# The first loads of a fused retention and SwiGLU kernel: constants moved to ScalarE's queue, their product moved behind the first scores, fewer unread products

## The chip, the cores and the metric

The kernel runs on one core of one Trainium2 chip. The core has TensorE (PE: products, PEld: its weight loads), VectorE (DVE), ScalarE (ACT), GpSimd (POOL) and SyncE (SP), which here only issues transfers; ScalarE can issue transfers too. The metric is the time of one execution on the device in microseconds (us), median of three runs.

## What is computed

Block-wise retention over 4 sequences of 768 rows with 8 heads of width 64, and then a gated feed-forward block (3072 rows, width 512, inner width 1536) over its output:

```python
for b in range(nb):                       # blocks of 64 rows
    qb, kb, vb = q[:, :, sl], k[:, :, sl], v[:, :, sl]
    intra = einsum('bhic,bhjc->bhij', qb, kb) * Dmask
    intra = einsum('bhij,bhjd->bhid', intra, vb)
    inter = einsum('bhid,bhde->bhie', qb * lam_pow, kv_state)
    out[:, :, sl] = intra + inter
    kv_state = lam_block * kv_state + einsum('bhsd,bhse->bhde', kb * rev_pow, vb)
...
rms = sqrt(mean(x * x, axis=-1) + 1e-6)
xn = x / rms * rms_g
g = xn @ w_gate
silu = g * (1.0 / (1.0 + exp(-g)))
return (silu * (xn @ w_val)) @ w_out
```

Here `lam` has one decay per head; `Dmask`, `lam_pow` and `rev_pow` are powers of it.

## The kernel before

**Tiling.** The 3072 rows are cut into 6 groups of 512. The heads are taken in 4 pairs, so a pair of heads fills 128 partitions. For each group and pair one tile `qkv` holds q and k across (half of the tile, called qK here) and k and v along (the other half, kv), each half 512 KB. The kernel uses chunks of 128 rows, four to a group.

**A pair's steps** (class `Pair`, lines 457 to 578). TensorE computes the scores `pa` from qK (line 477). VectorE multiplies them by the decay `mask` of each of the two heads into `a` (L497). ScalarE multiplies k by the last column of the masks (`decay_k`, L487). TensorE then makes the state sums `pst` from the decayed k and v (L510) and VectorE chains them into `state` (L523, L525). GpSimd multiplies q by `pw` (`decay_q`, L501). TensorE adds `a` times v and then the old state times the decayed q into `po` (`mix_chunks` L538, `mix_states` L549). ScalarE copies `po` away (`keep_output`, L561) and squares it (`keep_squares`, L572); GpSimd adds the squares of the first three pairs (L578), and TensorE sums them over the partitions into `pss` (L589) for the row norm.

**Constants.** A small tile `cs` (128 partitions of 64 bytes, 8 KB) holds the heads' decays and the norm's gain. VectorE makes from it eight masks (L153) and four `pw` (L158), each by a scan over 128 columns, and the largest gain `gmax` (L173), which TensorE spreads over the partitions by one product, `pmax` (L179); from that VectorE makes the scales `gs` (L183 to L189).

**Loads.** Before anything else the program issues `cs` (L67), the four pairs of group 0 (L96) and the first weights (L108). All go out from SyncE but one: the first pair's qK goes out from ScalarE (line 95). Both queues end in the same DMA engines. The pairs of the next group are issued from SyncE as soon as tiles come free.

**The order of the work** is written out by a planner (class `Plan`, lines 1089 to 1254). Each step has an engine, a cost, a due time, what it reads and writes. `arrive_steps` (line 1499) enters the landing of the first loads as steps with costs, `ramp_steps` (line 1510) the work on the first two groups. The table `SHIFTS` (line 1760) moves the due times of some 850 of 2730 steps. `Plan.run` goes through the steps and writes down, engine by engine, the order in which they are issued; on the chip each engine works through its instructions in that order and waits on semaphores.

**Unread products.** Where the planner sees TensorE idle for more than 0.8 us before the first Strassen unit, the loop at the end puts in products of the identity with itself, whose result nobody reads (`busy`, line 140; line 1969 sets how many). A product of float32 operands shows in the trace as two MATMUL records.

Of the kernel before, what the change touches and what calls it, by code (L numbers as in the profile page):

```python
# [22 lines left out]
def retention_swiglu_kernel(  # L23
# [11 lines left out]
    nc = tc.nc  # L35

    NG, NP = qkv.shape[:2]
# [28 lines left out]
    cs = const.tile([P, NC], F32, name="cs")  # L66
    nc.sync.dma_start(cs, consts)  # L67
# [55 lines left out]
    for p in range(NP):  # L123
        load_qkv(0, p)
# [1139 lines left out]
    step = plan.add  # L1264
# [234 lines left out]
    def arrive_steps():  # L1499
        def arrive():  # L1500
            pass

        step("LD", 4.3, -9, arrive, w=["cs", "come"])
        times = [0.75, 1.3, 1.55, 1.35, 1.85, 1.3, 1.3, 1.3]
        for p in range(NP):
            for i, c in enumerate(("qK", "kv")):
                step("LD", times[2 * p + i], -9, arrive, w=["come", *[f"q0_{p}:{x}" for x in c]])
        step("LD", 3.05, -9, arrive, w=["come", "gv0"])
# [234 lines left out]
    def load_steps():  # L1743
# [138 lines left out]
    with tc.manual_schedule(  # L1882
# [78 lines left out]
        for t, i in order:  # L1961
            eng, cost, _, fn, args, _, _, new, _ = plan.steps[i]
            begun = len(traced)
            if eng == "PE":
# [3 lines left out]
                if gaps and idle > 0.8:  # L1968
                    busy(int((idle - 0.5) / 0.24))
# [81 lines left out]
```

## Time and profile before

| | us |
|---|---|
| median of three runs | 631.17 (630.66 to 631.37) |
| profiled execution | 629.99 |
| its span, first to last instruction | 628.2 |
| TensorE busy in the span | 622.2 |

The profile is of one execution; its times start at the span's start. Busy time of TensorE is from modelled ends of its products, so a stretch in which it is busy throughout may still hold short waits. The rows that matter are in the section before the prediction.

### The profile page before, as it was taken

What the parts mean: (1) busy time and instruction counts of PE and PEld (TensorE: products, weight loads), DVE (VectorE), ACT (ScalarE), POOL (GpSimd) and SP (SyncE); (2) the same over time, 40 slices, a digit from 0 to 9 for tenths busy, and PEclk for the clock granted to TensorE, in tenths of its full rate; (3) what the DMA queues carried; (4) which work ended last, traced back from release to release, by engine and by line L of the source; (5) the groups of instructions that cost most, each with busy time, mean ns of one, the idle gap of its engine ahead of it and who ended that gap; (6) DMA issues with size and microseconds to landing.
All of it is one profiled execution on the core that took longest, in us unless ns stands there. A gap on an engine that the chain in (4) does not pass through costs nothing.

```text
span 628.2 us, 14174 instructions
## 1 busy us (share of the span) xinstructions
PE 622.2 (99%) x5665; PEld 479.3 (76%) x5665; DVE 452.8 (72%) x886; ACT 383.9 (61%) x724; POOL 127.6 (20%) x113
## 2 busy tenths in 40 slices
PE   9999999999999999999999999999999999999997
PEld 8864444455657777668888888888889888888886
DVE  6889888777787778788875789634874778546641
ACT  3779799986546764568764685534853564445531
POOL 3531201142825665410020110011000110000000
DMA  8899898888646788878878667744675667343401
GB/s 320 305 318 299 313 313 290 288 279 290 231 148 226 258 284 273 275 265 284 269 268 297 216 212 225 244 179 152 226 224 179 202 207 248 109 135 105 148 18 51
DMA packets 56033, 144.05 MB, mean 229 GB/s; under 512 B 5920, under 2 KB 18208, under 8 KB 54560
## 3 DMA queue, kind: packets, MB, share of 16 engines
q1 hardware_dynamic: 55824, 142.64, 67.3%
q8 instruction: 44, 0.72, 0.5%
q10 hardware_dynamic: 144, 0.52, 0.3%
q14 instruction: 21, 0.17, 0.1%
HBM read 106.96 MB, written 36.18 MB: 228 GB/s over the span
## 4 chain that ended last, share of the span: by engine, by line
PE 94%; DMA 2%; DVE 1%; ACT 1%; SPq 0%; issue 0%; POOL 0%; ACTq 0%; POOLq 0%
PE o L1050 20%; PE pa L779 20%; PE pb L779 15%; PE pv L668 9%; PE pg L668 9%; PE o L938 5%; PE pa L477 4%; PE po L538 3%; PE po L549 3%; DMA qkv<-in_qkv_dram 2%; PE o_own L1050 2%; PE pst L510 2%; PE pss L589 1%; PE unread L144 1%; PE pr L630 0%
## 5 line engine op out<-in xcount | busy, mean ns | idle before, releaser
L779 PEld LDWEIGHTS <-gw 128*128 128x128 f16 x1440 | 139.5, 98 | 21.9 <-issue 0.8
L1050 PE MATMUL o<-wo,late 128*128 128x256 f16 x1152 | 143.9, 273 | 0.5 <-ACT late L1061 0.5
L1050 PEld LDWEIGHTS <-late 128*128 128x128 f16 x1260 | 123.0, 98 | 15.1 <-issue 0.8
L668 PEld LDWEIGHTS <-w_half 128*128 128x128 f16 x576 | 53.9, 98 | 60.5 <-issue 1.5
L833 ACT COPY tx<-pa 128x256 f32<-128x256 f32 x96 | 35.3, 371 | 72.9 <-PE pa L779 55.5
L779 PE MATMUL pa<-tx,gw 128*128 128x256 f16 x576 | 77.4, 273 | 0.0
L668 PE MATMUL pv<-x,w_half 128*128 128x512 f16 x288 | 69.2, 379 | 0.2
L668 PE MATMUL pg<-x,w_half 128*128 128x512 f16 x288 | 66.8, 379 | 0.0
L837 DVE TENSOR_TENSOR tx<-pb,tx 128x256 f32<-128x256 f32 x96 | 40.0, 420 | 31.4 <-PE pb L779 29.1
L779 PEld LDWEIGHTS <-gv 128*128 128x128 f16 x576 | 56.0, 98 | 7.4 <-issue 0.2
L501 POOL TENSOR_TENSOR qkv<-qkv,pw 128x512 f32<-128x512 f32 x24 | 30.6, 1275 | 74.8 <-PE pa L477 66.5
L845 DVE TENSOR_TENSOR sg<-pb,sg 128x256 f32<-128x256 f32 x48 | 20.1, 422 | 35.4 <-ACT sg L841 30.7
L1013 DVE TENSOR_TENSOR late<-s,late 128x1024 f16<-128x1024 f32 x30 | 37.3, 1253 | 5.2 <-ACT late L1009 5.1
L708 POOL TENSOR_TENSOR r<-w_half 128x512 f32<-128x512 f16 x24 | 27.7, 1163 | 63.3 <-DVE w_half L440 25.5
L497 DVE TENSOR_TENSOR a<-pa,mask 128x512 f32<-128x512 f32 x48 | 31.4, 683 | 12.0 <-PE pa L477 8.5
L779 PE MATMUL pa<-x,gv 128*128 128x256 f16 x288 | 39.3, 273 | 0.0
L779 PE MATMUL pb<-x,gv 128*128 128x256 f16 x288 | 39.3, 273 | 0.0
L779 PE MATMUL pa<-x,gw 128*128 128x256 f16 x288 | 39.0, 273 | 0.0
L779 PE MATMUL pb<-tx,gw 128*128 128x256 f16 x288 | 39.0, 273 | 0.0
L779 PE MATMUL pb<-x,gw 128*128 128x256 f16 x288 | 38.7, 273 | 0.0
L938 PE MATMUL o<-wo,early 128*128 128x512 f16 x144 | 34.9, 379 | 0.0
L729 POOL TENSOR_TENSOR ws<-ws,ws 128x512 f16<-128x512 f32 x24 | 28.8, 1210 | 29.3 <-DVE en L325 15.3
(152 smaller groups left out, 1031.0 us busy)
## 6 DMA issues: line engine op xcount, KB each, us to landing
gw<-gw_kept SPq DMA_DIRECT2D x48, 640.0 KB, 4.8
qkv<-in_qkv_dram SPq DMA_DIRECT2D x47, 512.0 KB, 6.0
h<-h_kept SPq DMA_DIRECT2D x30, 512.0 KB, 4.1
h_kept<-sg SPq DMA_DIRECT2D x48, 256.0 KB, 3.4
gv<-gw_kept SPq DMA_DIRECT2D x48, 256.0 KB, 4.4
raw_gv<-in_weights_dram SPq DMA_DIRECT2D x11, 1024.0 KB, 7.2
raw_o<-in_weights_dram SPq DMA_DIRECT2D x24, 256.0 KB, 4.4
gw_kept<-ws SPq DMA_DIRECT2D x12, 512.0 KB, 4.2
```

The source lines that it names most:

```text
L477: nc.tensor.matmul(self.pa[j][:, c, :], self.kT[r, c, :], self.qT[r, c, :], start=True, stop=True,)
L497: nc.vector.tensor_mul(self.a[:, j], self.pa[j], decay)
L501: eng.tensor_mul(self.qT, self.qT, pw[:, p : p + 1, :].broadcast_to([P, GC, P]))
L668: nc.tensor.matmul(ps, w[:, kk, :], x[:, kk, :], start=i == kk == 0, stop=i == 2 and kk == NK - 1,)
L708: nc.gpsimd.tensor_add(self.r[:, i], w[:, 0], w[:, 1])
L729: eng.tensor_sub(self.to[:, c, 1], self.t[:, c], self.to[:, c, 0])
L779: nc.tensor.matmul(ps, w(ow, k), x(ox, k), start=first and i == k == 0, stop=i == 2 and k == 1, skip_group_check=True,)
L833: nc.scalar.copy(self.val_sums[:, self.half(t)], self.pa)
L837: nc.vector.tensor_add(v, self.pb, v)
L938: nc.tensor.matmul(self.banks[t], h[:, oh, t * P : (t + 1) * P], wo[:, j, 3 + 2 * k : 5 + 2 * k, ow], start=j == k == i == 0, stop=j == HA ...
L1013: eng.tensor_sub(lo, of, hi)
L1050: nc.tensor.matmul(bank[:, t], ops[:, oh, t * P : (t + 1) * P], w[:, ow], start=n in (1, 2, 5) and q == i == 0 and (t == 0 or bank is own) ...
```

## The change

The constants' transfer leaves the head of SyncE's queue, and is issued by ScalarE behind the first pair's qK. The planner's table of landings is replaced, with the landing of `cs` behind that of the first qK. The divisor that sets the number of unread products goes from 0.24 to 0.4. `SHIFTS` is replaced as a whole, which moves steps throughout the program.

```diff
     cs = const.tile([P, NC], F32, name="cs")
-    nc.sync.dma_start(cs, consts)
     lam_b, lam_p, gcol = cs[:, :H], cs[:, H : H + NP], cs[:, H + NP :]
...
-    for p in range(NP):
+    load_qkv(0, 0)
+    nc.scalar.dma_start(cs, consts)
+    for p in range(1, NP):
         load_qkv(0, p)
     load_gv(0)
...
-        step("LD", 4.3, -9, arrive, w=["cs", "come"])
-        times = [0.75, 1.3, 1.55, 1.35, 1.85, 1.3, 1.3, 1.3]
+        times = [5.0, 1.0, 1.6, 1.4, 1.6, 1.3, 1.3, 1.6]
         for p in range(NP):
             for i, c in enumerate(("qK", "kv")):
                 step("LD", times[2 * p + i], -9, arrive, w=["come", *[f"q0_{p}:{x}" for x in c]])
+                if p == i == 0:
+                    step("LD", 0.1, -9, arrive, w=["come", "cs"])
...
     SHIFTS = {
-        14: 13.03, 16: 14.75, 17: 15.55, 18: 16.43, 19: 19.96, 20: 21.25, 21: 18.22, 22: 18.97,
+        14: 13.01, 16: 14.72, 17: 15.58, 18: 16.46, 19: 20.01, 20: 21.3, 21: 18.25, 22: 19.03,
...
                 if gaps and idle > 0.8:
-                    busy(int((idle - 0.5) / 0.24))
+                    busy(int((idle - 0.5) / 0.4))
```

On TensorE, at the start of the program, the order before is this (`pa_0` are the scores of the first pair of heads, `pst_0` its state sums, `po_0` its output; `pa_1` and so on are the second pair's):

```order
L144 MATMUL unread<-ident 128x128 x10
L179 MATMUL pmax<-ident,gmax 128x128
L477 MATMUL pa_0_0_214<-qkv_0_145 128x128
...
L477 MATMUL pa_0_1_215<-qkv_0_145 128x128
L144 MATMUL unread<-ident 128x128 x3
L510 MATMUL pst_0_238<-qkv_0_145 64x64 x8
L538 MATMUL po_0_249<-a_0_228,qkv_0_145 64x128 x8
L477 MATMUL pa_1_0_262<-qkv_1_148 128x128
```

and of the changed kernel, at the same place, this:

```order
L145 MATMUL unread<-ident 128x128 x7
L478 MATMUL pa_0_0_205<-qkv_0_144 128x128
L478 MATMUL pa_0_1_206<-qkv_0_144 128x128
L478 MATMUL pa_0_0_205<-qkv_0_144 128x128
L478 MATMUL pa_0_1_206<-qkv_0_144 128x128
L180 MATMUL pmax<-ident,gmax 128x128
...
L511 MATMUL pst_0_227<-qkv_0_144 64x64 x8
L478 MATMUL pa_1_0_237<-qkv_1_148 128x128
...
L539 MATMUL po_0_245<-a_0_224,qkv_0_144 64x128 x4
```

The constants' product has moved from ahead of the first pair's scores into their middle, three unread products are gone ahead of them and three behind them, and the first half of the second pair's scores has moved ahead of the first pair's output. One more unread product, ahead of `pss`, is gone too: 14 before, 7 now.

On VectorE, at its first instructions, the order before is this (`mask` and `pw` are the scans over the constants, `a_0` the first pair's masked scores, the last row the second pair's):

```order
L173 TENSOR_REDUCE gmax<-cs 128x1
L153 SCALAR_TENSOR_TENSOR mask<-cs,ident 128x128 x2
L158 SCALAR_TENSOR_TENSOR pw<-cs,w_half_96 128x128
L153 SCALAR_TENSOR_TENSOR mask<-cs,ident 128x128 x2
L158 SCALAR_TENSOR_TENSOR pw<-cs,w_half_96 128x128
L153 SCALAR_TENSOR_TENSOR mask<-cs,ident 128x128
L497 TENSOR_TENSOR a_0_228<-pa_0_0_214,mask 128x512
L497 TENSOR_TENSOR a_0_228<-pa_0_1_215,mask 128x512
...
L153 SCALAR_TENSOR_TENSOR mask<-cs,ident 128x128 x2
L158 SCALAR_TENSOR_TENSOR pw<-cs,w_half_96 128x128
L497 TENSOR_TENSOR a_1_283<-pa_1_0_262,mask 128x512
```

and of the changed kernel this:

```order
L174 TENSOR_REDUCE gmax<-cs 128x1
L154 SCALAR_TENSOR_TENSOR mask<-cs,ident 128x128 x4
L159 SCALAR_TENSOR_TENSOR pw<-cs,w_half_95 128x128
L498 TENSOR_TENSOR a_0_224<-pa_0_0_205,mask 128x512
L498 TENSOR_TENSOR a_0_224<-pa_0_1_206,mask 128x512
L159 SCALAR_TENSOR_TENSOR pw<-cs,w_half_95 128x128
...
L498 TENSOR_TENSOR a_1_264<-pa_1_0_237,mask 128x512
L154 SCALAR_TENSOR_TENSOR mask<-cs,ident 128x128 x2
L159 SCALAR_TENSOR_TENSOR pw<-cs,w_half_95 128x128
L154 SCALAR_TENSOR_TENSOR mask<-cs,ident 128x128
L498 TENSOR_TENSOR a_1_264<-pa_1_1_238,mask 128x512
```

Five scans instead of seven stand ahead of the first pair's masked scores, and three masks and a `pw`, among them the mask that the second pair's second head waits for, have moved between the two halves of the second pair's masked scores.

On TensorE again, at the end of the four pairs of group 0 (`po_1` to `po_3` are their outputs, `pst` the state sums, `pss` the sums of squares for the norm), the order before is this:

```order
L538 MATMUL po_1_314<-a_1_283,qkv_1_148 64x128 x8
L549 MATMUL po_1_314<-qkv_1_148,state 64x128 x6
L477 MATMUL pa_3_0_335<-qkv_3_154 128x128
...
L510 MATMUL pst_2_342<-qkv_2_151 64x64 x8
L538 MATMUL po_2_353<-a_2_319,qkv_2_151 64x128 x8
...
L549 MATMUL po_2_353<-qkv_2_151,state 64x128 x6
L510 MATMUL pst_3_382<-qkv_3_154 64x64 x8
L538 MATMUL po_3_397<-a_3_379,qkv_3_154 64x128 x8
L144 MATMUL unread<-ident 128x128
L589 MATMUL pss_421<-ones,sq_304 128x1 x4
```

and of the changed kernel this:

```order
L539 MATMUL po_1_298<-a_1_264,qkv_1_148 64x128 x8
L478 MATMUL pa_2_0_276<-qkv_2_151 128x128
...
L550 MATMUL po_1_298<-qkv_1_148,state 64x128 x6
L511 MATMUL pst_2_327<-qkv_2_151 64x64 x8
L478 MATMUL pa_3_0_338<-qkv_3_154 128x128
...
L539 MATMUL po_2_356<-a_2_324,qkv_2_151 64x128 x8
L550 MATMUL po_2_356<-qkv_2_151,state 64x128 x6
L539 MATMUL po_3_382<-a_3_362,qkv_3_154 64x128 x8
L511 MATMUL pst_3_398<-qkv_3_154 64x64 x8
L590 MATMUL pss_411<-ones,sq_284 128x1 x4
```

The second half of the third pair's scores (`pa_2`) now stands behind the second pair's output, and the unread product ahead of `pss` is gone. On ScalarE, the constants' transfer has come in ahead of the table load, and the squares of the first and the third pair now stand ahead of the copies of their outputs.

## Rows read from the trace of the kernel before

**Rows 1.** The page's first part: busy time, share of the span and instructions of each engine.

```profile
PE 622.2 (99%) x5665; PEld 479.3 (76%) x5665; DVE 452.8 (72%) x886; ACT 383.9 (61%) x724; POOL 127.6 (20%) x113
```

**Rows 2.** Busy time by stretch: the stretch, its length, then busy time and instructions of PE, PEld, DVE, ACT and POOL, the granted TensorE clock, the share of the DMA engines and GB/s.

```profile
0.00:6.00 6.00, 4.54 (x22) 4.51 (x22) 1.20 (x5) 1.69 (x3) 1.41 (x11) 1.00 0.65 202
...
60.00:620.00 560.00, 559.53 (x4992) 432.97 (x4991) 402.97 (x771) 341.68 (x640) 106.36 (x86) 1.00 0.67 223
```

**Rows 3.** The timeline of TensorE from the start to 11.6 us: start, duration, engine, line, operation, out<-in, shapes, records, and in brackets the idle time before with what ended it.

```profile
1.46 4.48 PE L144 MATMUL unread<-ident 128*128 128x128 f32 x20 [1.46 <-POOL ident masks.py:199]
5.78 0.39 PE L179 MATMUL pmax<-ident,gmax 128*128 128x128 f32 x2
6.09 1.16 PE L477 MATMUL pa<-qkv 64*128 64x128 f32 x16
7.19 0.94 PE L144 MATMUL unread<-ident 128*128 128x128 f32 x6
8.05 0.68 PE L510 MATMUL pst<-qkv 128*64 128x64 f32 x16
8.57 1.15 PE L538 MATMUL po<-a,qkv 128*64 128x128 f32 x16
9.65 1.16 PE L477 MATMUL pa<-qkv 64*128 64x128 f32 x16
10.74 0.87 PE L549 MATMUL po<-qkv,state 64*64 64x128 f32 x12
```

**Rows 4.** The same timeline for the other engines and the two queues, same columns; ACTq and SPq are the issuing of transfers.

```profile
0.73 0.41 ACTq L96 DMA_DIRECT2D qkv<-in_qkv_dram  x1
0.74 0.39 SPq L67 DMA_DIRECT2D cs<-in_consts_dram  x1
...
4.80 0.16 DVE L173 TENSOR_REDUCE gmax<-cs 128x1 f32<-128x4 f32 x1 [4.80 <-DMA cs<-in_consts_dram]
4.88 0.73 DVE L153 TENSOR_TENSOR_SCAN mask<-cs,ident 128x128 f32<-128x128 f32 x2
...
6.76 0.91 ACT L487 ACTIVATE qkv<-qkv,mask 128x256 f32<-128x256 f32 x2 [3.90 <-DMA qkv<-in_qkv_dram]
...
7.29 1.29 DVE L497 TENSOR_TENSOR a<-pa,mask 128x512 f32<-128x512 f32 x2
...
9.40 0.91 DVE L525 SCALAR_TENSOR_TENSOR state<-state,pw,pst 128x64 f32<-128x64 f32 x3
```

**Rows 5.** Single transfers: of the answers for the moments 0.74, 1.15 and 1.7 us, the issue row of SyncE where it is not among rows 4 (start, duration), and the transfer's row (out<-in, queue, count, KB, us from the start of its issue to its landing). The first two rows are the first pair's qK and the constants, the next two the first pair's kv, the last two the second pair's qK.

```profile
qkv<-in_qkv_dram ACTq DMA_DIRECT2D x1, 512.0 KB, 4.7
cs<-in_consts_dram SPq DMA_DIRECT2D x1, 8.0 KB, 4.0
...
1.18 0.42 SPq L96 DMA_DIRECT2D qkv<-in_qkv_dram  x1
qkv<-in_qkv_dram SPq DMA_DIRECT2D x1, 512.0 KB, 5.5
...
1.65 0.42 SPq L96 DMA_DIRECT2D qkv<-in_qkv_dram  x1
qkv<-in_qkv_dram SPq DMA_DIRECT2D x1, 512.0 KB, 6.3
```

**Rows 6.** What the DMA engines moved for each queue (q10 is ScalarE's, q1 SyncE's): packets, MB, share of 16 engines' time; the first row is the stretch 1.7 to 2.1 us, the next three 2.1 to 4.1 us, the last two 4.1 to 5.3 us.

```profile
q1 hardware_dynamic: 61, 0.00, 8.4%
...
DMA packets 188, 0.44 MB, mean 221 GB/s; under 512 B 81, under 2 KB 81, under 8 KB 188
q10 hardware_dynamic: 107, 0.43, 90.0%
q1 hardware_dynamic: 81, 0.01, 3.0%
...
q1 hardware_dynamic: 100, 0.39, 79.7%
q10 hardware_dynamic: 34, 0.08, 20.0%
```

**Rows 7.** The timeline from 17.8 to 22.4 us, all engines, columns as in rows 3: the end of the four pairs of group 0.

```profile
17.86 0.87 PE L549 MATMUL po<-qkv,state 64*64 64x128 f32 x12
...
18.78 0.58 ACT L561 COPY x<-po 128x512 f32<-128x512 f32 x1 [1.71 <-PE po L549]
...
19.26 0.60 ACT L572 ACTIVATE sq<-po 128x512 f32<-128x512 f32 x1
...
19.75 1.15 ACT L209 ACTIVATE w<-w_half 128x1024 f32<-128x1024 f32 x1
...
20.00 1.27 POOL L578 TENSOR_TENSOR sq<-sq,sq 128x512 f32<-128x512 f32 x1 [0.68 <-ACT sq L572]
...
20.32 0.49 PE L144 MATMUL unread<-ident 128*128 128x128 f32 x2
...
21.28 0.68 DVE L216 TENSOR_SCALAR w<-w 128x1024 int32<-128x1024 int32 x1
...
21.33 1.05 PE L589 MATMUL pss<-ones,sq 128*128 128x1 f32 x8 [0.53 <-POOL sq L578]
```

**Rows 8.** The list of waits, TensorE alone, whole span: who waited for whom, us in total, times, longest.

```profile
PE pss L589 <- POOL sq L578: 0.5, 1, 0.5
PE o L1050 <- ACT late L1061: 0.5, 1, 0.5
```

233 rows, old and new, of the table SHIFTS are left out of this document.

## The prediction

> **What bounds the kernel now.** I read the page first, then busy time by stretch, the list of waits, the timeline of the first 24 us, and last single transfers and the packets of each queue. The page has TensorE busy for 99% of the span [rows 1]; the stretches say where the rest is: from 60 to 620 us it is busy for 559.53 of 560 us [rows 2], and beside the start its list of waits has two of 0.5 us [rows 8]. So the time is a chain of TensorE's work, and what the change can move is when that chain gets going. From about 22 us on it passes a shift on, as long as the engines that feed it are shifted as much or have slack.
>
> The start of that chain, before: ten unread products run from 1.46 to 5.94 us, then `pmax`, then the first scores from 6.09 [rows 3]. The scores' qK had landed at 0.73 + 4.7 = 5.43, the constants at 0.74 + 4.0 = 4.74, kv at 1.18 + 5.5 = 6.68 [rows 4, 5]. So the first scores came 0.66 later than their data. ScalarE's `decay_k` started at 6.76, on kv's landing, and ended at 7.67; three unread products ended at 8.13, and the state sums started at 8.05 [rows 3, 4]. VectorE started at 4.80 on the constants and had seven scans done by 7.29, when it took up the masked scores: 0.34 each at most [rows 4]. The place where the pairs of group 0 end is `pss` at 21.33, which waited for GpSimd's sum of squares, and that for ScalarE's squares [rows 7].
>
> **The change part by part.**
>
> *Unread products.* One costs 4.48/10 = 0.45 us at the start, 0.94/3 = 0.31 later [rows 3]. Seven end at 1.46 + 7 x 0.448 = 4.60, ahead of qK. With `pmax` behind the first half, the scores start when qK is there, at 5.5, instead of 6.09: 0.6 earlier. The three behind the scores held TensorE until 8.13 where k was ready at 7.67: gone, 0.4 earlier. The one at 20.32 ran while TensorE waited for GpSimd [rows 7]: nothing. This is up to 0.6 us off TensorE's own order, if nothing else is late at the first pair's output.
>
> *kv first on SyncE's queue.* It is issued at 0.74 instead of 1.18 [rows 4, 5]: 6.24 instead of 6.68 if it takes its 5.5 again. At best it lands with qK, at 5.4; at worst as before, if qK beside it takes the engines. `decay_k` then waits for the masks, not for kv.
>
> *Constants behind qK.* This is the part that pays. Say they land at L (4.74 before). VectorE's first scan starts 0.14 behind L [rows 4]; five scans stand ahead of the masked scores now, so these start at L + 0.14 + 5 x 0.34 = L + 1.84 and end 1.29 later at L + 3.1 [rows 4]. Then come, up to the end of the second pair's masked scores, six scans (2.0), a copy and three state steps (0.91 for three, so 1.2) and the scores' 1.29 [rows 4]: 4.5, so L + 7.6. VectorE has no gap in this as far as L is late. Behind it TensorE has, in its new order, `po_1`, half of `pa_2`, `mix_1`, `pst_2`, `pa_3`, `po_2`, `mix_2`. By differences of starts a `po` is 1.08, a `pa` 1.09, a `mix` 0.80, a `pst` 0.52 [rows 3]: 1.08 + 0.55 + 0.80 + 0.52 + 1.09 + 1.08 + 0.80 = 5.9, so `mix_2` ends at L + 13.5 or, with some 0.1 for the handing over, L + 13.6.
>
> *Squares ahead of the copy.* Before, ScalarE started the copy at 18.78 and ended the squares at 19.86, 1.08 later [rows 7]. With the squares first it is 0.60 + 0.05, a gain of 0.4. From the squares' end to `pss` it was 21.33 - 19.86 = 1.47. So `pss` starts at L + 13.6 + 0.65 + 1.47 = L + 15.7, against 21.33: the break-even is L = 5.6, and each 0.1 us of L behind that costs 0.1.
>
> *What L is.* No row shows a small transfer behind a large one of its own queue, so I bound it. Below: not before qK, whose queue it shares, 5.43, which gives -0.2. Above: from 2.1 to 4.1 us the constants' last 81 packets and 107 packets of qK shared the engines, two whole us [rows 6]. If the small ones again take 2.0 us, now beside SyncE's large ones and after qK's data (which ends inside the stretch 4.1 to 5.3, at perhaps 4.4 by its 34 packets), and land 4.74 - 4.1 = 0.64 behind their last packet, L is 7.0: +1.4. I take 5.6. The nearest row is that of the constants themselves: they landed 0.7 from a transfer 64 times their size that had started with them, so their time is set by what runs with them and not by their bytes, and 61 of 144 packets had gone in 0.4 us [rows 6]. That gives 0 at `pss`.
>
> The Trainium skill, "DMA: Bandwidth & Descriptors", section "Queues, rings and completion order", says that each DMA engine takes turns between the queues that have work for it, and drains a whole packet of some 9 to 17 descriptors before it switches. If that packet is a transfer's whole share of an engine, the constants would go in one turn, behind qK and at most one share of kv, and the sum would be near the low bound; the mixing of 81 with 107 records agrees with it only if different engines began with different queues, which these rows can't tell.
>
> *Weights.* ScalarE's lift of the first weights now stands behind the later copy: at L = 5.6 `mix_2` ends at 19.2, squares and copy at 20.4, the lift at 21.6 instead of 20.9. VectorE took the lift's result up at 21.28, 0.38 after it was ready [rows 7]. So up to 0.3 could be lost there; TensorE waits for it only through a later product, with a step of group 1 between. Between nothing and 0.3, I take nothing.
>
> *The replaced table.* The rest of the program has the same instructions in another order. There TensorE's waits sum to 0.47 us of 560 [rows 2]: that much can be won, and one input that comes late can lose more. I take nothing, with 0.5 to either side.
>
> **Sum.** Nothing at `pss`, nothing behind: the profiled execution stays at 629.99 us (628.2 of span and 1.8 around it). It lies 1.2 below the median of the runs, 631.17, and the median is what is predicted: 631.2. A run can tell no change from a change beyond some 0.2%, 1.26 us here; all terms but the latest L lie inside that.
>
> **The rivals.**
>
> *A, slower: the constants come a whole turn late.* VectorE can't start its masks, and all four pairs of group 0 stand behind it. For it: the two us of shared packets. Against it: the first 61 went at once. At L = 6.7 it costs 1.1 us, 632.3; at 7.0 it is 632.6. It decides from L = 5.6 on, and passes 0.2% at L = 6.9.
>
> *B, faster: the first transfers gain.* From 2.1 to 4.1 us the engines moved 0.44 MB, 221 GB/s, with 81 small packets among them; from 4.1 to 5.3 it was 0.47 MB, 392 GB/s [rows 6]. Without small packets in that stretch the stream would be 2.0 x (392 - 221) = 0.34 MB ahead, 0.9 us of the later rate. If the constants share in it, L is near 5.0 and `pss` 0.6 earlier: 630.6; with half a us from the later order, 630.1. Against it: the engines may have been slow to start for any reason, and the small packets still come, only later.
>
> *C, slower: TensorE runs slow at first.* An unread record took 0.224 us in the first run of them and 0.157 in the second [rows 3], a factor of 1.43, though the granted clock reads 1.00 from the start [rows 2], the level of 2.4 GHz. With a gap from 4.60 to 5.5 the early pace might last. If it lasts to the end of `mix_0`, its products (1.09 + 0.22 + 0.52 + 1.09 + 1.08 + 0.80 = 4.8 us) take 2.1 more; VectorE's chain covers about half of it: +1.0, 632.2. The Trainium skill, "TensorE: Matmul & The Clock Gate", Part 1, says that the clock is low by default and that activity releases it, which speaks against taking unread products away; the granted clock of these rows shows no low level.
>
> *D: the later order wins or loses.* Half a us less if both waits go, 630.7; about 1.3 more if a load comes late, 632.5.
>
> **Chances.** The forecast, within 0.6 us of no change, 0.53 (its own range 630.5 to 631.9); A 0.20; B 0.14; C 0.04; D 0.09. Faster by over 0.2%: half of B, a third of D, a little of the forecast, 0.14. Slower by over 0.2%: two fifths of A, half of C, a third of D, and a little of the forecast, 0.16. Within 0.2%: 0.70. The range takes in most of A and B: 629.9 to 632.7.
>
> **What would show it.** The first VectorE instruction gives L at once: at 5.5 to 5.8 the forecast, at 6.5 or more A, at 5.1 or less B. The masked scores then start 1.8 behind it, and `pss` 15.6 behind it. The first scores should start at 5.5 with a gap ahead of them, records of 0.068 us as before; slower ones show C. TensorE's waits from 60 to 620 us over 1.3 or a `pss` that keeps its place while the span changes show D. The forecast is wrong if `pss` lies more than 0.6 us from 21.3, or if it doesn't and the time moves all the same.

## The result, and the profile after

The change made the kernel slower: 636.26 us (median of 7 runs, 634.06 to 639.39) against 631.07 us for the kernel before, run beside it (7 runs, 630.16 to 633.17), a ratio of 1.0088 with a 95% interval of 1.0064 to 1.0112. The forecast was 631.2 in a range up to 632.7. The runs also lie further apart: 5.3 us from lowest to highest, 3.0 before.

The profiled execution of after took 637.98 us, with a span of 635.8. Its page, in the part that answers to [rows 1]:

```profile
PE 624.2 (98%) x5651; PEld 479.9 (75%) x5651; DVE 454.8 (72%) x886; ACT 383.4 (60%) x724; POOL 128.8 (20%) x113
```

TensorE has 14 instructions fewer (the unread products) and is busy 2.0 us longer. The same products took longer somewhere. The stretches, for TensorE alone, name one suspect and at once seem to clear it (stretch, length, busy time, granted clock, DMA share, GB/s; answers to [rows 2]):

```profile
0.00:6.00 6.00, 3.60 (x16) 1.00 0.67 240
25.00:60.00 35.00, 34.44 (x351) 1.00 0.84 294
60.00:600.00 540.00, 536.54 (x4766) 1.00 0.70 231
```

The granted clock reads 1.00 throughout, the level of 2.4 GHz. For the first row that is a trap. The column is worked out from the clock records of the trace and counts a time without a record as full. The first record of after's trace starts at 14.43 us (full clock, 1.00); ahead of it there is none. The trace of before has no clock record at all, so the 1.00 of [rows 2] said nothing of its start either.

From 60 to 600 us, TensorE now stands idle for 3.46 us; before it was at most 0.47 [rows 2]. From 25 to 60 us it is 0.56, where before has 0.26:

```profile
25.00:60.00 35.00, 34.74 (x325) 1.00 0.86 294
```

The timeline of the start shows the rest (it answers to [rows 3, 4]: start, duration, engine, line, operation, and in brackets the idle time before with what ended it):

```profile
1.47 3.36 PE L145 MATMUL unread<-ident 128*128 128x128 f32 x14 [1.47 <-POOL ident masks.py:199]
5.75 1.23 PE L478 MATMUL pa<-qkv 64*128 64x128 f32 x8 [0.93 <-DMA qkv<-in_qkv_dram]
...
7.76 0.16 DVE L174 TENSOR_REDUCE gmax<-cs 128x1 f32<-128x4 f32 x1 [7.76 <-DMA cs<-in_consts_dram]
...
7.97 0.80 PE L180 MATMUL pmax<-ident,gmax 128*128 128x128 f32 x2 [0.99 <-DVE gmax L174]
...
9.86 1.12 PE L511 MATMUL pst<-qkv 128*64 128x64 f32 x16
9.96 1.29 DVE L498 TENSOR_TENSOR a<-pa,mask 128x512 f32<-128x512 f32 x2 [0.45 <-PE pa L478]
...
14.27 0.71 PE L539 MATMUL po<-a,qkv 128*64 128x128 f32 x8
14.37 0.69 DVE L498 TENSOR_TENSOR a<-pa,mask 128x512 f32<-128x512 f32 x1 [1.41 <-PE pa L478]
```

Two things stand there. VectorE starts on the constants at 7.76 instead of 4.80. And eight score records take 1.23 us where sixteen took 1.16 before; a `pst` takes 1.12 instead of 0.68. Only at 14.27 do eight `po` records take 0.71, the pace that TensorE had from 6.09 on before. That is where the first clock record starts: the slow pace ends with the first recorded full clock. That the slow pace is the lower level, 1.2 GHz, a recorded stretch of run e3 shows (below). VectorE waited for the slow scores twice, 0.45 and 1.41 us.

The end of group 0 (answers to [rows 7]) has the outcome of both:

```profile
22.17 0.87 PE L550 MATMUL po<-qkv,state 64*64 64x128 f32 x12
...
23.09 0.60 ACT L573 ACTIVATE sq<-po 128x512 f32<-128x512 f32 x1 [1.66 <-PE po L550]
...
24.05 1.15 ACT L210 ACTIVATE w<-w_half 128x1024 f32<-128x1024 f32 x1
...
25.17 1.05 PE L590 MATMUL pss<-ones,sq 128*128 128x1 f32 x8 [0.63 <-POOL sq L579]
25.23 0.69 DVE L217 TENSOR_SCALAR w<-w 128x1024 int32<-128x1024 int32 x1
```

`pss` starts 25.17 - 21.33 = 3.84 us later. The list of TensorE's waits (answers to [rows 8]) has two behind it that are longer than anything before:

```profile
PE pa L780 <- ACT sg L850: 1.5, 1, 1.5
PE pn L421 <- DVE en L326: 1.4, 1, 1.4
```

So the profiled execution's 7.99 us are: 3.84 up to `pss`; from 25 to 600 us an idle time of 0.56 + 3.46 = 4.02 where it was 0.26 + 0.47 = 0.73, which is 3.29 more; and some 0.9 at the end and outside the span that I haven't followed.

Why the constants were late, the transfers and packets tell (they answer to [rows 5, 6]; the first three rows are KB and us from issue to landing for kv, the first pair's qK and the constants; then the packets, MB and share of ScalarE's queue, q10, from 5.3 to 7.3 us, and of both queues from 5.3 to 6.3 us):

```profile
qkv<-in_qkv_dram SPq DMA_DIRECT2D x1, 512.0 KB, 4.8
...
qkv<-in_qkv_dram ACTq DMA_DIRECT2D x1, 512.0 KB, 5.0
...
cs<-in_consts_dram ACTq DMA_DIRECT2D x1, 8.0 KB, 6.6
...
q10 hardware_dynamic: 143, 0.01, 4.7%
...
q1 hardware_dynamic: 93, 0.36, 93.3%
q10 hardware_dynamic: 84, 0.01, 5.7%
```

Between 5.3 and 6.3 us ScalarE's queue moved 84 packets with 0.01 MB, and SyncE's 93 with 0.36 MB. The small packets went about one for one with the large ones instead of passing between them. By the packet records the small ones started from 5.27 to 7.22 us, and the time from one small packet to a later one is most often 0.16 us, which is what one large packet takes (0.159): as if on each engine one large packet stood between two small ones.

### The profile page after: what moved, and what is told of

Its sections match the earlier page's. It is cut to its first block, busy times and chain, and to the rows that moved or that the text cites. A ratio compares the mean times of both kernels' runs of the same rounds, so it can differ in the third digit from the quotient of the medians.

```text
span 635.8 us, 14160 instructions
## 1 busy us (share of the span) xinstructions
PE 624.2 (98%) x5651; PEld 479.9 (75%) x5651; DVE 454.8 (72%) x886; ACT 383.4 (60%) x724; POOL 128.8 (20%) x113
## 4 chain that ended last, share of the span: by engine, by line
PE 86%; DMA 5%; DVE 4%; ACT 3%; issue 1%; SPq 0%; ACTq 0%
PE o L1051 20%; PE pa L780 19%; PE pb L780 14%; PE pv L669 7%; PE pg L669 7%; PE o L939 4%; PE pa L478 4%; PE po L539 3%; PE po L550 3%; DMA qkv<-in_qkv_dram 2%; PE o_own L1051 2%; PE pst L511 2%; DMA w_kept<-wo_f 1%; DMA cs<-in_consts_dram 1%; PE pss L590 1%
## 5 line engine op out<-in xcount | busy, mean ns | idle before, releaser
L850 ACT ACTIVATE sg<-sg,cg 128x256 f32<-128x256 f32 x48 | 24.3, 507 | 18.6 <-DVE sg L846 18.4
```

## The experiments

Three causes were in question: the later constants, TensorE's slow pace, and the replaced order. The ten runs are of nine kernels (e10 repeats e5), the table says what each takes from before and from after. The kernel before had medians of 630.92 (29 runs) beside the first four, 631.3 (22 runs) beside the next three and 631.3 (29 runs) beside the last three.

| kernel | order | constants | unread at the start | median us (runs) | ratio to before, 95% interval | `pss` at |
|---|---|---|---|---|---|---|
| before | before | first, SyncE | 10 | 631.07 (7) | | 21.33 |
| after | after | behind qK | 7 | 636.26 (7) | 1.0064 to 1.0112 | 25.17 |
| e1 | after | first, SyncE | 7 | 632.20 (10) | 0.9996 to 1.0036 | 20.93 |
| e2 | before | behind qK | 10 | 636.14 (8) | 1.0050 to 1.0095 | 26.06 |
| e3 | before | first, SyncE | 6 | 632.85 (10) | 1.0001 to 1.0045 | 22.53 |
| e4 | after | behind qK | 12 | 634.13 (10) | 1.0032 to 1.0059 | 22.90 |
| e5 | after | first, SyncE | 10 | 633.44 (12) | 1.0016 to 1.0044 | 21.17 |
| e6 | after | behind kv, SyncE | 12 | 633.08 (7) | 1.0010 to 1.0044 | 21.27 |
| e7 | before | behind qK | 14 | 634.21 (6) | 1.0030 to 1.0066 | 23.72 |
| e8 | before to 27 us, then after | first, SyncE | 10 | 632.68 (12) | 0.9992 to 1.0029 | 21.09 |
| e9 | after to 27 us, then before | first, SyncE | 10 | 631.49 (12) | 0.9974 to 1.0012 | 21.51 |
| e10 | after | first, SyncE | 10 | 633.34 (12) | 0.9994 to 1.0035 | 21.54 |

**The constants back at the head (e1).** The changed kernel, its loads undone:

```diff
+    nc.sync.dma_start(cs, consts)
...
-    load_qkv(0, 0)
-    nc.scalar.dma_start(cs, consts)
-    for p in range(1, NP):
+    for p in range(NP):
         load_qkv(0, p)
```

> The changed kernel with the constants' transfer put back at the head of SyncE's queue; everything else (order, seven unread products) as changed. Theory 1 (late constants): the constants land at about 4.7 again instead of 7.74, VectorE starts at 4.8, and the products for the row norm start near 21 instead of 25.2; about 632. Theory 2 (TensorE's slow pace after the gap that the missing unread products leave): seven products still end near 4.8, the pace stays low through the first pairs, and the norm's products start at 22 to 23; about 633.5. Theory 3 (the new order of the rest costs most): the waits at about 102 and 322 us stay; 634 or more.

632.20 us: some 4 us come back. TensorE's start (as in the timeline above):

```profile
4.87 1.22 PE L477 MATMUL pa<-qkv 64*128 64x128 f32 x8
...
6.47 0.72 PE L477 MATMUL pa<-qkv 64*128 64x128 f32 x8
```

The same seven unread products take the same 3.36 us, but qK is there when they end, so TensorE goes on without a pause and has its full pace by the second half of the scores (the first clock record starts at 6.12). `pss` is 0.4 earlier than before, and yet the kernel is no faster: what is gained at the start is lost behind it. With the changed order and the fewer unread products left, that was the first sign against the order.

**The loads alone (e2).** The kernel before with the changed loads (that part of the diff alone).

> The kernel before with only the loads moved as in the change (k and v first on SyncE, constants behind q and K on ScalarE); order and fourteen unread products as before. Theory 1: the constants land at 7.5 to 7.8, the first scores stand behind the constants' product at about 8, the norm's products at about 24; 633 to 634.5. Theory 2: ten unread products bring the pace up before the gap, so no slow products; the loss is what VectorE's late start costs, 2 us, 633. Theory 3: no change, 631.

636.14 us, as slow as after. Here the order of before puts the constants' product ahead of all scores:

```profile
7.74 0.80 PE L180 MATMUL pmax<-ident,gmax 128*128 128x128 f32 x2 [1.64 <-DVE gmax L174]
8.47 2.08 PE L478 MATMUL pa<-qkv 64*128 64x128 f32 x16
```

TensorE stands for 1.64 us, and the sixteen score records take 2.08 instead of 1.16; the first clock record starts at 13.84. By itself this run can't tell late constants from slow pace; it led to e7.

**Fewer unread products alone (e3).** Before, with six ahead of `pmax`, two behind the scores and none later:

```diff
-                    busy(int((idle - 0.5) / 0.24))
+                    busy(int((idle - 0.5) / 0.4))
```

> The kernel before with only the divisor changed: six unread products at the start instead of ten, two behind the scores instead of three, none ahead of the norm's products. Theory 2: the gap before the first scores (4.2 to 5.5, with the constants' product in it) leaves TensorE at its low pace for some us; the scores' eight products take 2.0 to 2.5 us instead of 1.16, and the norm's products come 1 to 2 us later; 632 to 633. Theory 1: nothing changes by more than 0.5 us, 631; the first scores start at 5.5.

632.85 us, with the constants where they were (VectorE at 4.76):

```profile
4.98 0.80 PE L179 MATMUL pmax<-ident,gmax 128*128 128x128 f32 x2 [0.58 <-DVE gmax L173]
5.70 2.08 PE L477 MATMUL pa<-qkv 64*128 64x128 f32 x16
...
10.85 1.16 PE L477 MATMUL pa<-qkv 64*128 64x128 f32 x16
...
23.52 2.01 PE L477 MATMUL pa<-qkv 64*128 64x128 f32 x16
```

The scores start 0.4 earlier than in [rows 3] and end 0.5 later. With a pause of 0.58 us TensorE kept its half pace; the first clock record starts at 9.98, and by 10.85 it had the full one. Taking out products that nobody reads cost 1.2 us at `pss`.

In this profile the clock also fell again behind that. No unread product stands ahead of `pss` here, TensorE waited 0.95 us for it, and from 23.63 to 27.04 us the trace records a clock of 0.50 (here the column shows it: stretch, length, busy time, granted clock, DMA share, GB/s):

```profile
23.60:27.10 3.50, 3.50 (x32) 0.51 0.42 165
```

The sixteen score records in that stretch take 2.01 us, as the first ones did: the slow pace is the level of 1.2 GHz. Seven of e3's ten executions have a mean granted clock of 0.997, of before's 29 beside it four have less than 0.999.

**More unread products in after (e4).** The mirror image: after, twelve at the start instead of seven.

```diff
-                    busy(int((idle - 0.5) / 0.4))
+                    busy(int((idle - 0.5) / 0.24))
```

> The changed kernel with the old divisor: twelve unread products at the start instead of seven (to about 6.9), all else as changed. Theory 2: the pace is full from the first scores on, the norm's products start at about 23.4 instead of 25.2; 634.5. Theory 1: VectorE still starts at 7.8 and the norm's products move by less than 0.5 us; 636. Theory 3: 636.

634.13 us, 2.1 less than after, with the constants as late as there:

```profile
1.47 5.49 PE L145 MATMUL unread<-ident 128*128 128x128 f32 x24 [1.47 <-POOL ident masks.py:199]
...
7.55 0.16 DVE L174 TENSOR_REDUCE gmax<-cs 128x1 f32<-128x4 f32 x1 [7.55 <-DMA cs<-in_consts_dram]
...
8.18 0.72 PE L478 MATMUL pa<-qkv 64*128 64x128 f32 x8
```

Five products more at the start, which themselves delay the first scores by 1.1 us (6.89 against 5.75), bring `pss` 2.3 us earlier, and the first clock record from 14.43 to 7.20. That is the pace, and it is shown: nothing else in the kernel differs, though 0.2 of the 2.3 may be the constants, which came that much earlier in this execution. After's two waits of 1.5 and 1.4 us are 0.3 or less here, in the same order; what made them long in after's profile stays open.

**The order alone (e5, and e10 again).** Before's loads and ten unread products, but the changed order (e1 with the divisor at 0.3).

> The changed order alone: the kernel before's loads, ten unread products ahead of the first scores, everything else in the changed kernel's order. If the new order itself costs (the constants-first run reached the norm's products 0.4 us earlier than the kernel before and still ended 1.3 us later): the norm's products start at 21 to 21.5, some waits of TensorE come between 60 and 300 us, total 632 to 632.5. If the order costs nothing and what the constants-first run lost was its slow first scores: 631.

> The same kernel as e5_order_alone, for a profile of a typical execution: the earlier profile was of a run of 631.8 where the median was 633.4. Both theories expect a median of 633.2 to 633.7. If the later order loses in waits for inputs that come late, a profile of 633 or more has waits of TensorE beside the start that sum to 2.5 us or more, against 2.1 in the profile of 631.8 and 1.0 in that of before; if its waits are no longer, TensorE's products themselves took longer.

633.44 and 633.34 us: 2.0 to 2.1 us above before, with `pss` at its old place. e5's profile was of one of its fastest executions (631.79). e10's, of 632.81, has more waits than before had, none longer than 0.6 us: behind the first two pairs its list sums to 2.8 us, against 1.0 in before. I had asked for 2.5 in a profile of 633 or more, so that agrees, though the profile is a little short of 633. The largest sum is this:

```profile
PE pst L510 <- ACT qkv L487: 0.7, 2, 0.4
```

e10's interval against before still takes in 1; e5's doesn't.

**The two halves of the order (e8, e9).** The planner's list of steps is cut at 27 us; e8 has before's list up to there and after's for the rest, e9 the opposite, both with before's loads and ten unread products. `REST` is the other list without the steps that are done.

```diff
-        order = plan.run()
+        order = [x for x in plan.run() if x[0] < 27.0]
+        order += [(27.0, i) for i in REST]
```

> The kernel before, with its own loads, unread products and order for the first 120 steps (those that the planner starts ahead of 27 us: group 0's scans and the first weights), and the changed kernel's order for the 2,611 steps behind them. If what the changed order costs (2.1 us of median with the loads of before) lies in the later order, this gives 632.9 to 633.6 (ratio 1.0025 to 1.0035) with pss at 21.3 as before and group 1's norm spread no later than 62.8 us; if it lies in the order of the start, 631.0 to 631.6 (ratio 0.9995 to 1.0005). A mixed answer, 631.9 to 632.5, would say that either part costs something.

> The opposite half: loads of before, ten unread products, the changed order for the first 122 steps and the order of before for the 2,609 behind them. If the later order is what costs, this is level with the kernel before, 631.0 to 631.6, or as much as 0.4 better, since pss came 0.1 to 0.4 earlier with the changed order of the start (20.9 and 21.2 against 21.3); if the order of the start costs, 632.9 to 633.6.

e8 gave 632.68, e9 631.49: by medians 1.4 and 0.2 us above before. The runs of before beside them lay wide (629.4 to 636.4), so that neither interval excludes 1; and 1.4 lies between the answers that I had set down for the later order and for a mixed cause. Set against each other the runs say more: e9 and e10 have the same loads, the same unread products and the same order up to 27 us, and were run on the same chip. Behind that, e10 has after's order, and its twelve executions are 1.84 us longer by means (95% interval 1.1 to 2.6). The later order costs; this shows it. Where, the traces tell. TensorE alone from 25 to 60 and 60 to 600 us, e8 first:

```profile
25.00:60.00 35.00, 33.67 (x319) 1.00 0.86 290
60.00:600.00 540.00, 537.87 (x4795) 1.00 0.70 230
```

and e9:

```profile
25.00:60.00 35.00, 34.62 (x324) 1.00 0.85 291
60.00:600.00 540.00, 539.09 (x4802) 1.00 0.69 230
```

Idle are 3.46 us in e8, 1.29 in e9, 0.73 in before. e8's span is 2.5 us longer than before's; its idle time is 2.7 more and its `pss` 0.2 earlier, so the waits explain it. They are these:

```profile
PE pst L510 <- ACT qkv L487: 1.6, 3, 0.7
...
PE pa L779 <- DMA gw<-gw_kept: 1.3, 1, 1.3
```

The first can be followed to the order for 1.33 of its 1.6 us. ScalarE and TensorE near 41 us in before:

```profile
40.53 0.91 ACT L487 ACTIVATE qkv<-qkv,mask 128x256 f32<-128x256 f32 x2 [0.75 <-DMA qkv<-in_qkv_dram]
...
41.47 0.58 PE L510 MATMUL pst<-qkv 128*64 128x64 f32 x12
```

and in e8:

```profile
41.14 0.51 ACT L487 ACTIVATE qkv<-qkv,mask 128x256 f32<-128x256 f32 x1 [1.51 <-DMA qkv<-in_qkv_dram]
41.55 0.61 ACT L416 ACTIVATE junk<-w 128x512 bf16<-128x512 f32 x1
...
42.17 0.49 ACT L487 ACTIVATE qkv<-qkv,mask 128x256 f32<-128x256 f32 x1
...
41.70 0.33 PE L510 MATMUL pst<-qkv 128*64 128x64 f32 x2 [0.65 <-ACT qkv L487]
42.71 0.56 PE L510 MATMUL pst<-qkv 128*64 128x64 f32 x10 [0.68 <-ACT qkv L487]
```

In the changed order a weight's squares (`junk`) stand between the two halves of `decay_k`; with k 0.6 later as well, the state's products stop twice.

**Full pace with late constants, order of before (e7).** e2 with fourteen unread products at the start, so that TensorE works until the constants are there:

```diff
-                    busy(int((idle - 0.5) / 0.24))
+                    busy(14 if t < 6 else int((idle - 0.5) / 0.24))
```

> The loads alone (kernel before with the changed loads) with fourteen unread products at the start instead of ten, so that TensorE works until the constants are there; the order is that before. If the gap ahead of the constants' product is what keeps TensorE slow: the sixteen score records take 1.2 us instead of 2.08, the norm's products start at 23.5 to 24 instead of 26.1, total 633.5 to 634; what is left against the kernel before, some 2.5 us, is then VectorE's late start alone. If the pace has to do with the loads or with something else: slow products again, 636.

634.21 us, 1.9 less than e2 (2.3 less, each taken against the kernel before run beside it). The pause is 0.24 instead of 1.64, and the scores have their old pace; the first clock record starts at 6.78, ahead of the pause:

```profile
7.62 0.49 PE L180 MATMUL pmax<-ident,gmax 128*128 128x128 f32 x2 [0.24 <-DVE gmax L174]
8.04 1.16 PE L478 MATMUL pa<-qkv 64*128 64x128 f32 x16
```

The 2.9 us that stay above before are the price of the changed loads with full pace under before's order (interval 1.9 to 4.2); `pss` is 2.4 later.

**The constants behind kv on SyncE's queue (e6).** e4 with the small transfer on the other queue, behind another transfer of 512 KB:

```diff
     load_qkv(0, 0)
-    nc.scalar.dma_start(cs, consts)
+    nc.sync.dma_start(cs, consts)
```

> The run with twelve unread products, with the constants' transfer behind the first k and v on SyncE's queue instead of behind q and K on ScalarE's. If the constants are late because their small packets take turns with another queue's large ones: ScalarE's queue is empty once q and K are through, so the small packets go at once, and the constants land at 6.0 to 6.5 instead of 7.5; the norm's products start at about 21.8; about 633. If small packets are slow behind a large transfer whatever the other queue does: they land at 7.3 or later, and nothing changes, 634.

```profile
cs<-in_consts_dram SPq DMA_DIRECT2D x1, 8.0 KB, 4.7
```

They land 4.7 us after their issue, not 6.4 as in e4, and VectorE starts at 5.92 instead of 7.55. The large transfer ahead is of the same size; what differs is what the other queue holds. The packets of e4 from 5.8 to 6.3 us:

```profile
q1 hardware_dynamic: 44, 0.16, 97.9%
q10 hardware_dynamic: 44, 0.00, 6.0%
```

and of e6 from 5.1 to 5.4 us:

```profile
q1 hardware_dynamic: 123, 0.12, 114.0%
q10 hardware_dynamic: 8, 0.00, 1.5%
```

Behind qK on ScalarE's queue (q10) the small packets face SyncE's, where the other pairs' six transfers are still to come: 44 to 44 in half a us. Behind kv on SyncE's (q1) they face ScalarE's, which has no more than qK and has all but finished it: 123 go in 0.3 us, most of them small. `pss` is back at 21.27, and the kernel still takes 633.08: about what the order alone costs.

No kernel beat the one before; e9 is level with it.

## Why the prediction was wrong

**L, the constants' landing: the term that was mis-sized first.** Predicted 5.6, bounds 5.43 to 7.0; measured 7.7, outside them. I took the value near the constants' own row, because 61 of 144 packets had gone in 0.4 us [rows 6]. That only showed how fast they go with nothing beside them; beside SyncE's large packets they took 5.27 to 7.22, 1.95 us. The upper bound had this right, 2.0 us, though by luck: the 2.0 us were those of 81 packets, and at that rate 144 take 3.6. What the bound had wrong is the end of qK's data, put at 4.4 and measured at 5.3: 0.9 more, less 0.05 for the packets and 0.15 for the landing, make 7.7 of 7.0. The rule from the Trainium skill, "DMA: Bandwidth & Descriptors", section "Queues, rings and completion order", that an engine drains a whole packet of some 9 to 17 descriptors before it switches, spoke for the low bound as I had read it; 84 small records beside 93 large in a us, with starts most often 0.16 us apart, don't agree with that reading, and e6 against e4 shows that the time depends on what the other queue holds.

**`pss` = L + 15.7: right, as far as TensorE has its pace.** e4, with VectorE's start at 7.55 and so L = 7.49, gives 23.2; it was at 22.90. After gives 23.4 and was at 25.17: 1.8 more, where e4's extra products removed 2.3. The step that failed there is "VectorE has no gap in this as far as L is late": it waited 0.45 and 1.41 us for TensorE's slow scores, 1.86 together.

**Unread products cost nothing to remove: wrong.** Seven ended at 4.83, the scores came at 5.75 and not at 5.5, with a pause of 0.93. That the early pace might last was rival C, with 1.0 us and a chance of 0.04. It lasted to 14 us and cost 2.1 us of median (after against e4, and 1.9 by e2 against e7). I set it low because the granted clock read 1.00, and that reading was wrong: the trace of before has no clock record, and the column counts what isn't recorded as full. The first sentences of the Trainium skill's rule that I had cited, "TensorE: Matmul & The Clock Gate", Part 1, pointed the right way, and the traces agree: the first recorded full clock starts at 4.3 to 14.4 us, and in after eight score records go from 1.23 to 0.72 there. The factor between the first and second unread runs [rows 3] was there to be weighed: it was the mean of a run that held both paces.

**kv first: better than said.** It took 4.8 and landed at 5.54, inside its bounds and below the 6.24 taken. It gained nothing, since `decay_k` waited for the masks, as predicted; and qK beside it took 5.0, where it took 4.1 to 4.7 with the loads of before, which is why the scores came at 5.75.

**Squares ahead of the copy: right.** From the end of `mix_2` to `pss` it is 25.17 - 23.04 = 2.13; the terms, 0.65 and 1.47, made 2.12. **Lift and weights: right** as nothing that shows: VectorE takes the lift up at 25.23, right when it ends, and e9, which has the changed start, is level with before.

**The replaced table: nothing, with 0.5 to either side. Wrong.** It costs 2.0 to 2.1 us by e5 and e10, most of it in the later order (e8 1.4, e9 0.2 by medians; e10 against e9 1.84 by means). The row was read rightly, 0.47 us of waits in 560 leave little to win; but then the error can't be the same to both sides. An order that has no waits has only one way to go. Rival D named it, a load that comes late, at 1.3 us and one part of 0.09; e8's `gw` came 1.3 late. In after's own profile the two longest waits were for ScalarE and VectorE, not for a load.

**Rivals A, C and D came together.** I had made each a case of its own, and added its price to a kernel otherwise unchanged: at most 632.6. With the prices given (1.4, 1.0, 1.3) the sum of all three would have been 634.9. By runs, each against the kernel before run beside it, the path is: order +2.1 (e5), late constants with full pace +1.1 (e4 less e5), slow pace +2.0 (after less e4), a chain of differences that ends at the 5.2 measured. Under before's order the late constants cost 2.9 (e7). So by medians the changed order hides about 1.8 us of the delay that comes with it, and costs about as much by itself; with intervals of some 1 us to either side of each, how much it hides isn't settled. Nor is why single executions of the changed order differ by up to 4 us. One thing that differs is on record: the same twelve unread products took 5.49 us in e4's profile and 4.28 in e6's, where the first clock record starts at 7.20 and at 4.30.

All the signs that I had named for A, C and D were there: first VectorE instruction past 6.5, slower score records, waits over 1.3 from 60 to 620 us.

## What to carry to other kernels

A small transfer that shares the DMA engines with large ones of another queue can't be priced by its bytes: here it went packet for packet with them, so look at its packets and at what the other queue holds. (No run changed the number of its packets.) A first-needed constant goes first, or on a queue that has nothing large against it. Work that nobody reads can be what carries TensorE to its pace: compare the duration of one form early and late before taking it out, and ask whether a clock column that stays at 1.00 has a record behind it. And where the trace shows an order almost free of waits, a new order is a risk to one side, to be added to the other terms and not weighed against them.

## What the runs showed of the hardware

- The granted clock column reads 1.00 also where the trace has no clock record. None of these traces has one before 4.3 us. Ahead of the first one eight score records took 1.22 to 1.23 us (after, e1), and 0.71 to 0.72 from the first record on, which is of the full clock. Sixteen took 2.01 in a stretch recorded at 0.50 (e3), 2.08 early in e2 and e3, 1.16 at 1.00.
- Where TensorE didn't stand between its first unread product and the first recorded full clock, that clock starts at 4.3 to 7.2 us (e1, e4 to e10). Where it stood for 0.58 us (e3), 0.93 and 0.99 (after) or 1.64 (e2), it starts at 9.98, 14.43 and 13.84. The number of products ahead isn't what tells these apart: after and e1 have seven, e2 and e5 ten. e7's pause of 0.24 us came after the rise.
- Later pauses differ. After 0.95 us ahead of e3's `pss` the clock was recorded at 0.50 from 23.63 to 27.04; after 0.63 ahead of after's `pss`, and 1.4 and 1.5 later, the record stays at 1.00.
- A transfer of 8 KB in packets of 64 bytes took 3.1 to 4.0 us at the head of a queue, 4.7 behind 512 KB when the other queue ran out (e6), and 6.2 to 6.6 behind 512 KB when it didn't (after, e2, e4, e7).
